# Holding the transposed loads of x behind the first chunk's copies, readying the gate column sooner, and loading the first two transposed chunks in one transfer

## The chip, the cores and the metric

The kernel runs on one core of one Trainium2 chip. The metric is the device time of one execution in microseconds (us).

## The reference, cut to what matters

```python
# A_x: (1, 2048, 640) bf16; the rows are worked on in 16 chunks of 128
def _A_ref(x, wqkv, wo):
    qkv = x @ wqkv                      # q, k, v, 32 heads of 20
    pq, pk = phi(q), phi(k)             # phi(t) = (t > 0 ? t + 1 : exp(t)) + 1e-6
    kv = einsum("bhsd,bhse->bhde", pk, v); z = sum of pk over s
    o = (pq @ kv) / (pq @ z + 1e-6)
    return o @ wo
def _B_ref(x, w1, w2, w3, w4): ...      # layernorm, gelu, shifted mixing, a second gelu block
g = sigmoid((x * gate_w).sum(-1))
return g * _A_ref(x) + (1 - g) * _B_ref(x)
```

The change touches only the first stage: k = x @ wk for each chunk of x, with the logit of the gate as one more column.

## The kernel before

In profiles and code, PE is TensorE (PEld its weight loads), DVE the vector engine, ACT the scalar engine; SP, and ACT as well, issue DMA transfers. A transfer lands when all its data have arrived. To evacuate a result is to take it out of PSUM, the memory that TensorE writes.

For k, TensorE needs each chunk of x transposed (xT). Chunks 0 and 1 are loaded plainly and transposed by TensorE itself (`turn`); DVE copies the results from PSUM into xT. Chunks 2 to 15 come transposed by DMA (`load_xT`). The weights wk come in five parts of 128 rows, by two issuing queues (SP and ACT).

```python
    load_x(0, 1)                                             # SP
    aq.dma_start(g5[:], gate_w.rearrange("(c p) -> c p", p=P))   # ACT
    load_wk(sp, 1)
    load_wk(aq, 0)
    load_x(1, 2, aq)
    load_wk(sp, 3)
    load_wk(aq, 2)
    load_wk(sp, 4)
    for c0, c1 in ((2, 3), (3, 4), (4, 6), (6, 8), (8, 12), (12, 16)):
        load_xT(c0, c1)                                      # SP, transposing
    sp.dma_start(wq_sb, wqkv_v[:, :, 0:D])
    load_x(2, 8)
    # ... cut: the other loads, all on SP
    # ... cut: constants
    def k_mm(pt, c, dcs, first=0, last=DC - 1):
        for dc in dcs:
            for hf in range(2):
                n = HD + hf                  # 320 and 321: the last column is the gate's logit
                nc.tensor.matmul(pt[:, hf, 0:n], lhsT=xT[:, dc, c * P:(c + 1) * P],
                                 rhs=wk_sb[:, dc, hf * HD:hf * HD + n], start=(dc == first), stop=(dc == last))
    # ... cut
    k0_order = (1, 0, 3, 4, 2)
    # ... cut: warmup(n, w) issues matmuls of constants, to bring TensorE to full pace
    turns = [(pair(), a, b) for a, b in ((0, 2), (2, DC))]

    def turn(c):
        for pt, a, b in turns:
            # ... cut: matmuls of x_sb[:, c, ...] against the identity
            if c == 0 and b == DC:
                nc.tensor.matmul(pt[:, 1, 0:DC], lhsT=g5z[:], rhs=ident[:, 0:DC], start=True, stop=True)
            nc.vector.tensor_copy(xT[:, a:b, c * P:(c + 1) * P], ...)
            if c == 0 and b == DC:
                nc.vector.tensor_copy(wk_sb[:, :, D], pt[:, 1, 0:DC])      # the gate column

    turn(0)
    warmup(1, TS)
    for n, dc in enumerate(k0_order):
        if n == 3:
            turn(1)
        elif 1 <= n < 3:
            warmup(1, 2 * P)
        k_mm(kp, 0, (dc,), first=k0_order[0], last=k0_order[-1])
    k_evac(kp, 0)
    for c in range(1, NCH):
        pt = pair()
        k_mm(pt, c, range(DC))
        k_evac(pt, c)
```

## Time and profile before

| | |
|---|---|
| time, median of 3 runs | 264.57 us (264.44 to 264.81) |
| span of the profiled execution | 262.6 us |
| TensorE busy | 98% of the span |
| first x transpose issued | 2.65 us |
| chunk 1's first k matmul | 6.99 us |
| chunk 2's first k matmul | 8.35 us |

The page of the kernel before: the first part gives the busy time of each engine with its share of the span, the fourth the share of the chain of work that ended last.

```profile
PE 257.9 (98%) x1719; PEld 160.0 (61%) x1738; DVE 142.7 (54%) x282; ACT 82.7 (31%) x123; POOL 20.2 (8%) x65
...
PE 98%; issue 0%; DVE 0%
```

TensorE is busy nearly everywhere, and the chain is TensorE's own order. So a change among the loads can only matter where TensorE waits for one of them. That is at the start. The next lines are the timeline of the kernel before: start, duration (both us; lines merge neighbours of one kind), engine, source line, operation, what it writes and reads, and in brackets the idle time before it with what ended it.

```profile
2.65 9.69 SPq L122 DMA_TRANSPOSE xT<-in_A_x_dram  x5
...
3.13 0.57 PEld L216 LDWEIGHTS <-x_sb 128*128 128x128 bf16 x5 [0.49 <-DMA x_sb<-in_A_x_dram]
...
3.69 0.89 DVE L219 CAST xT<-pp 128x256 bf16<-128x256 f32 x2 [1.28 <-PE pp L216]
...
4.22 0.93 PE L186 MATMUL pp<-wk_sb,xT 128*128 128x320 bf16 x2
4.49 0.17 DVE L222 CAST wk_sb<-pp 128x5 bf16<-128x5 f32 x1
...
5.15 0.68 PE L186 MATMUL pp<-wk_sb,xT 128*128 128x320 bf16 x2
...
5.77 0.44 PE L186 MATMUL pp<-wk_sb,xT 128*128 128x320 bf16 x2
6.08 0.28 PEld L214 LDWEIGHTS <-x_sb 128*128 128x128 bf16 x5 [0.20 <-DMA x_sb<-in_A_x_dram]
...
6.44 3.84 PE L186 MATMUL pp<-wk_sb,xT 128*128 128x320 bf16 x27
```

The six transposes are issued from 2.65 us on. The copy of the gate column (L222) ends at 4.66 us. TensorE transposes chunk 1 from 6.08 us, after a wait for its load, and from 6.44 us it runs k matmuls without a gap. Single records in the trace give the spacing: 320 columns take 0.27 us up to about 5.6 us and 0.136 us afterwards. I call these half and full pace. Chunk 1 then starts at 6.99 us and chunk 2 at 8.35 us. The pages have one trap: a matmul's record is about 300 ns long while matmuls start every 136 ns. So records overlap, and a short hole between them shows less idle time than it costs. Delays below are read from start to start.

### The profile page before, as it was taken

The numbers are of one execution on the slowest core, as the hardware profiler recorded it, in microseconds if no ns is written. First come the engines' busy times: TensorE is split into PE (matmuls) and PEld (weight loads), VectorE is DVE, ScalarE is ACT, GpSimd is POOL, SyncE is SP. The second block draws the span as 40 slices with busy tenths as digits, with TensorE's granted clock in tenths as the row PEclk, the third lists the DMA queues.
The fourth block names the chain that finished last, engine by engine and source line by source line (L and its number), as shares of the span: only waits on it lengthen the run. The fifth ranks groups of instructions, "written<-read, shape, count | busy, mean of one in ns | idle before, by whom it ended". The sixth has DMA issues, their size and how long they took to land.

```text
span 262.6 us, 4246 instructions
## 1 busy us (share of the span) xinstructions
PE 257.9 (98%) x1719; PEld 160.0 (61%) x1738; DVE 142.7 (54%) x282; ACT 82.7 (31%) x123; POOL 20.2 (8%) x65
## 2 busy tenths in 40 slices
PE   8999999999999999999999999999999999999995
PEld 4777555788755644555577555567565577555553
DVE  2788778899947998955403464413356223112132
ACT  1555554321166236522502222412131332142200
POOL 5000050012210040001000001000001000000000
DMA  7999987016682566600132000051100051100011
GB/s 204 197 171 379 364 248 304 0 27 125 125 99 58 111 121 167 235 0 2 25 75 77 25 0 2 0 100 52 50 0 2 1 100 52 50 0 2 0 50 50
DMA packets 45757, 23.98 MB, mean 91 GB/s; under 512 B 35114, under 2 KB 44970, under 8 KB 45738
## 3 DMA queue, kind: packets, MB, share of 16 engines
q1 hardware_dynamic: 45296, 23.22, 35.1%
q10 hardware_dynamic: 442, 0.49, 0.5%
q8 instruction: 13, 0.21, 0.4%
q14 instruction: 6, 0.05, 0.1%
HBM read 12.21 MB, written 2.62 MB: 56 GB/s over the span
## 4 chain that ended last, share of the span: by engine, by line
PE 98%; issue 0%; DVE 0%
PE pp L500 22%; PE pp L467 21%; PE pp L186 9%; PE pp L315 8%; PE pp L451 8%; PE pp L420 8%; PE pp L349 8%; PE pp L243 8%; PE pp L199 1%; PE pp L387 1%; PE pp L475 1%; PE pp L509 1%; PE pp L368 1%; PE pp L258 0%; PE pp L216 0%
## 5 line engine op out<-in xcount | busy, mean ns | idle before, releaser
L467 PE MATMUL pp<-lnxT,w_sb 128*128 128x512 bf16 x249 | 59.8, 379 | 0.6
L500 PE MATMUL pp<-w_sb,h 128*128 128x384 bf16 (+3 forms) x414 | 57.6, 299 | 0.2 <-issue 0.2
L469 ACT ACTIVATE h<-pp 128x1024 bf16<-128x1024 f32 (+1 forms) x28 | 26.9, 961 | 82.2 <-PE pp L467 82.2
L500 PEld LDWEIGHTS <-h 128*128 128x128 bf16 x416 | 38.3, 98 | 19.3 <-issue 1.1
L467 PEld LDWEIGHTS <-w_sb 128*128 128x128 bf16 x260 | 25.4, 98 | 26.8
L514 DVE SCALAR_TENSOR_TENSOR oc<-pp,omg,x 128x640 bf16<-128x640 f32 (+2 forms) x20 | 14.4, 748 | 45.1 <-ACT h2x L478 21.3
L454 DVE SCALAR_TENSOR_TENSOR x<-pp,gate,x 128x640 f32<-128x640 f32 x16 | 13.9, 868 | 29.4 <-PE pp L451 29.4
L178 ACT ACTIVATE e<-pp 128x640 bf16<-128x640 f32 (+1 forms) x26 | 21.5, 826 | 9.6 <-PE pp L243 9.6
L451 PE MATMUL pp<-m_sb,pqT 128*128 128x320 bf16 x160 | 24.3, 299 | 0.0
L420 PE MATMUL pp<-w_sb,hsT 128*128 128x320 bf16 x160 | 23.9, 299 | 0.0
L423 DVE TENSOR_TENSOR x<-pp,x_sb 128x640 f32<-128x640 f32 x16 | 13.1, 820 | 19.7 <-PE pp L420 19.7
L186 PE MATMUL pp<-wk_sb,xT 128*128 128x320 bf16 (+1 forms) x160 | 23.1, 303 | 0.0
L315 PE MATMUL pp<-x_sb,pk 128*128 128x320 bf16 (+1 forms) x160 | 22.0, 300 | 0.0
L243 PE MATMUL pp<-xT,hsT 128*128 128x512 bf16 x98 | 21.6, 379 | 0.1
L315 PEld LDWEIGHTS <-pk 128*128 128x128 bf16 x160 | 18.8, 117 | 3.2
L420 PEld LDWEIGHTS <-hsT 128*128 128x128 bf16 x160 | 15.7, 98 | 8.2
L451 PEld LDWEIGHTS <-pqT 128*128 128x128 bf16 x160 | 15.7, 98 | 7.7
L186 PEld LDWEIGHTS <-xT 128*128 128x128 bf16 x160 | 15.7, 99 | 6.5 <-DVE xT L219 0.2
L349 PE MATMUL pp<-lnxT,w_sb 128*128 128x512 bf16 x76 | 17.9, 379 | 0.2
L243 PEld LDWEIGHTS <-hsT 128*128 128x128 bf16 x100 | 11.8, 118 | 9.7
L285 POOL TENSOR_SCALAR rstd<-mv 128x4 f32<-128x4 f32 (+1 forms) x11 | 3.4, 312 | 153.6 <-DVE mv L291 153.6
L180 DVE SCALAR_TENSOR_TENSOR pk<-pp,e 128x640 bf16<-128x640 f32 x16 | 13.2, 825 | 1.7
(76 smaller groups left out, 189.9 us busy)
## 6 DMA issues: line engine op xcount, KB each, us to landing
out_dram<-oc SPq DMA_DIRECT2D x14, 160.0 KB, 1.8
w_sb<-in_B_w_dram SPq DMA_DIRECT2D x1, 2160.0 KB, 8.4
w_sb<-in_B_w_dram SPq DMA_DIRECT2D x1, 2080.0 KB, 9.9
x_sb<-in_A_x_dram SPq DMA_DIRECT2D x1, 1280.0 KB
x_sb<-in_A_x_dram SPq DMA_DIRECT2D x1, 960.0 KB, 7.4
wo_sb<-in_A_wo_dram SPq DMA_DIRECT2D x6, 160.0 KB, 7.8
hsT<-in_A_wqkv_dram SPq DMA_DIRECT2D x1, 800.0 KB, 5.1
m_sb<-in_A_wqkv_dram SPq DMA_DIRECT2D x1, 800.0 KB, 12.0
```

The source lines that it names most:

```text
L178: nc.scalar.activation(ev, src, ACT.Exp)
L186: nc.tensor.matmul(pt[:, hf, 0:n], lhsT=xT[:, dc, c * P:(c + 1) * P], rhs=wk_sb[:, dc, hf * HD:hf * HD + n], start=(dc == first), stop=(dc ...
L243: nc.tensor.matmul(pt[:, t % 2, :], lhsT=wq_sb[:, dc, :].rearrange("p (m j) -> p j m", j=DC)[:, j], rhs=xT[:, dc, t * TS:(t + 1) * TS], st ...
L315: nc.tensor.matmul(pt[:, hf, 0:HD + hf], lhsT=w, rhs=x_sb[:, c, hf * HD:(hf + 1) * HD + hf], start=(c == 0), stop=(c == NCH - 1))
L349: nc.tensor.matmul(pt[:, i, :], lhsT=w, rhs=lnxT[t][:, dc, :], start=(dc == 0), stop=(dc == DC - 1))
L420: nc.tensor.matmul(pt[:, hf, 0:HD], lhsT=hsT[:, fc, 2 + c * P:2 + (c + 1) * P], rhs=w2_sb[:, fc, hf * HD:(hf + 1) * HD], start=(fc == 0), ...
L451: nc.tensor.matmul(pt[:, hf, 0:HD], lhsT=pqT[:, j, c * P:(c + 1) * P], rhs=m_sb[:, j, hf * HD:(hf + 1) * HD], start=(j == 0), stop=(j == D ...
L454: nc.vector.scalar_tensor_tensor(x1, pt[:, :, 0:HD], gate[:, c:c + 1], x1, op0=ALU.mult, op1=ALU.add)
L467: nc.tensor.matmul(pt[:, k, :], lhsT=w3_sb[:, dc, fc * P:(fc + 1) * P], rhs=lnT[:, dc, :], start=(dc == 0), stop=(dc == DC - 1))
L469: nc.scalar.activation(h2[:, 2 * i * TS:(2 * i + n) * TS], pt[:].rearrange("p h e -> p (h e)")[:, 0:n * TS], ACT.Gelu_apprx_tanh)
L500: nc.tensor.matmul(dst, lhsT=st[t]["h2"][:, fc * TS + cc * P:fc * TS + (cc + 1) * P], rhs=w4_sb[:, fc, a:b], start=start and fc == 0, stop ...
L514: nc.vector.scalar_tensor_tensor(oc[:, a:b], src, omg[:, c:c + 1], st[t]["x1"][cc][:, a:b], op0=ALU.mult, op1=ALU.add)
```

## The change

The intent: keep the transposes and all later loads off the DMA engines until chunk 0's first copies are done, so that the plain loads at the start are not disturbed; get the gate column ready sooner; and bring chunks 2 and 3 in one transfer (chunks 8 to 11, one transfer before, become two pairs). The hold is a one-column memset inside chunk 2's place in xT. The transpose that overwrites it must wait for DVE, and everything behind it on the SP queue waits too.

```diff
-    for c0, c1 in ((2, 3), (3, 4), (4, 6), (6, 8), (8, 12), (12, 16)):
-        load_xT(c0, c1)
-    sp.dma_start(wq_sb, wqkv_v[:, :, 0:D])
-    ... (the later loads)
+
+    def late_loads():
+        for c0, c1 in ((2, 4), (4, 6), (6, 8), (8, 10), (10, 12), (12, 16)):
+            load_xT(c0, c1)
+        sp.dma_start(wq_sb, wqkv_v[:, :, 0:D])
+        ... (the later loads, in the same order)
@@ in turn(c)
-            if c == 0 and b == DC:
+            if c == 0 and a == 0:
                 nc.tensor.matmul(pt[:, 1, 0:DC], lhsT=g5z[:], rhs=ident[:, 0:DC], start=True, stop=True)
             nc.vector.tensor_copy(xT[:, a:b, c * P:(c + 1) * P], ...)
-            if c == 0 and b == DC:
+            if c == 0 and a == 0:
                 nc.vector.tensor_copy(wk_sb[:, :, D], pt[:, 1, 0:DC])
+                nc.vector.memset(xT[:, 0:1, 2 * P:2 * P + 1], 0.0)
 
     turn(0)
+    late_loads()
+    ... (POOL's copies of w1, which need a late load, moved here unchanged)
     warmup(1, TS)
```

More of the change, by code (lines that the diff above doesn't have):

```diff
@@ L134 @@
     load_wk(sp, 4)
-    for c0, c1 in ((2, 3), (3, 4), (4, 6), (6, 8), (8, 12), (12, 16)):
-        load_xT(c0, c1)
-    sp.dma_start(wq_sb, wqkv_v[:, :, 0:D])
-    load_x(2, 8)
-    load_x(8, 16)
-    sp.dma_start(wv_sb[:], wqkv_v[:, :, 2 * D:3 * D])
-    sp.dma_start(w1_sb[:], B_w1.rearrange("(c p) f -> p c f", p=P))
-    for g in range(NG):
-        sp.dma_start(wo_sb[:, g, :], A_wo[row0[g]:row0[g] + P, :])
-    for g in range(4):
-        sp.dma_start(w2_sb[:, g, :], B_w2[CG * g:CG * g + P, :])
-        sp.dma_start(w2_sb[32 * g:32 * (g + 1), 4, :], B_w2[CG * g + P:CG * (g + 1), :])
-    sp.dma_start(w3_sb[:], B_w3.rearrange("(c p) f -> p c f", p=P))
+    def late_loads():
+        for c0, c1 in ((2, 4), (4, 6), (6, 8), (8, 10), (10, 12), (12, 16)):
+            load_xT(c0, c1)
+        sp.dma_start(wq_sb, wqkv_v[:, :, 0:D])
+        load_x(2, 8)
+        load_x(8, 16)
+        sp.dma_start(wv_sb[:], wqkv_v[:, :, 2 * D:3 * D])
+        sp.dma_start(w1_sb[:], B_w1.rearrange("(c p) f -> p c f", p=P))
+        for g in range(NG):
+            sp.dma_start(wo_sb[:, g, :], A_wo[row0[g]:row0[g] + P, :])
+        for g in range(4):
+            sp.dma_start(w2_sb[:, g, :], B_w2[CG * g:CG * g + P, :])
+            sp.dma_start(w2_sb[32 * g:32 * (g + 1), 4, :], B_w2[CG * g + P:CG * (g + 1), :])
+        sp.dma_start(w3_sb[:], B_w3.rearrange("(c p) f -> p c f", p=P))
     nc.gpsimd.memset(mhalf[:], -0.5)
@@ L167 @@
         nc.gpsimd.memset(kvT[:, b:b + 2], 0.0)
-    for dc in range(DC):
-        for g in range(4):
-            nc.gpsimd.tensor_copy(w1x[:, dc, 32 * g:32 * (g + 1)], w1_sb[:, dc, CG * g + P:CG * (g + 1)])
     def phi(dst, src, n):
@@ L220, in turn @@
                                   ptb[:, 0:(b - a) * P].rearrange("p (c s) -> p c s", c=b - a))
-            if c == 0 and b == DC:
+            if c == 0 and a == 0:
                 nc.vector.tensor_copy(wk_sb[:, :, D], pt[:, 1, 0:DC])
+                nc.vector.memset(xT[:, 0:1, 2 * P:2 * P + 1], 0.0)
     turn(0)
+    late_loads()
+    for dc in range(DC):
+        for g in range(4):
+            nc.gpsimd.tensor_copy(w1x[:, dc, 32 * g:32 * (g + 1)], w1_sb[:, dc, CG * g + P:CG * (g + 1)])
     warmup(1, TS)
```

## The prediction

> **What bounds it now.** TensorE. The page's first part has PE busy 257.9 of 262.6 us, and the chain that ended last is 98% PE. Later stages are dense, so the change can act only on the first ten microseconds and on when the transposed chunks arrive.
>
> The timeline of the first 9 us shows:
> - x chunk 0 lands at 3.1 us; its identity matmuls run 3.2 to 3.8 us, then two DVE casts (423 and 547 ns) and a 169 ns copy of the gate column into wk_sb (4.49 to 4.66 us).
> - The first chunk's second matmul needs that column and starts only at 4.72 us, 0.5 us after the first. Matmuls run at half pace until about 5.6 us (320 columns every 0.27 us, later every 0.136).
> - Chunk 1's transposes start at 6.08 us, when x chunk 1 lands. From 6.99 us PE is unbroken at 1.36 us a chunk: chunk 2 at 8.35 us, chunk 4 at 11.1.
>
> The x transposes are issued at 2.65, 4.0, 5.3, 6.8, 8.5 and 12.4 us. Chunk 2 lands near 6.45 us (3.8 after issue), chunk 3 at 7.8, chunks 4-5 at 9.7 (4.4 after issue), 6-7 at 12.0: 1.3 to 1.9 us of slack. In the trace's packets the transposes start to move at 5.3 us and share the engines with the last 100 or so of 896 row packets of the plain loads.
>
> **What the change does.**
> 1. The gate-column matmul and copy move to the first half of chunk 0: ready near 4.4 us instead of 4.66, PE gains 0.25 us. The second cast ends 0.45 us later (near 5.0), needed near 5.5: free.
> 2. A one-column DVE memset (0.1 us) in chunk 2's place makes the first transpose wait: issued near 4.6 us instead of 2.65, with all that is behind it on the SP queue.
> 3. Without transposes in the way x chunk 1 and the last two wk parts (6.03, 6.40, 6.58 us) land about 0.3 us sooner. PE would reach chunk 2 at 8.1 us: the gain of 0.25 us is kept.
> 4. Chunks 2-3 come in one transfer. Chunks 4-5 took 4.4 us behind a backlog; single lnxT chunks later, without traffic, take 2.6. My estimate for the pair is 3.6 to 4.4 us, landing 8.2 to 9.0. Chunk 2's slack is spent: PE waits 0.1 to 0.9 us, most likely 0.5.
> 5. Later pairs, issued every 1.55 us, land near 10.4, 12.5, 14.5 and 16.5 us, needed near 11.2, 14, 16.7, 19.4: no second wait. The queue gets to wq near 17 us as now (16.7; wq lands at 21.8, needed at 27.4).
>
> **Sum.** -0.25 us from the gate column, +0.5 us from the wait at chunk 2: about +0.2 us. A wait under 1 us should not bring back the half pace: the Trainium skill ("TensorE: Matmul & The Clock Gate", Part 1) has the clock drop after an idle window of about 3.4 us. The trace before has no such idle stretch to test it on.
>
> **Predicted 264.7 us, 8 in 10 within 263.9 to 265.5.** Chances: faster by over 2% 0.01, within 2% 0.98, slower by over 2% 0.01.
>
> **What would show it.** First transpose issued near 4.6 us; second matmul of chunk 0 near 4.5; x chunk 1 landing near 5.7; PE idle some 0.5 us before chunk 2, released by the x transpose; no other gap; later stages shifted as one block.
>
> **What would make it wrong.** If the pair lands in 3.4 us there is no wait and the time is about 264.3. If it takes over 5 us, the wait exceeds 1 us and half pace might come back, costing a microsecond or more. TensorE reaching full pace sooner or later because its start changed: half a microsecond either way.

## The result, and the profile after

The changed kernel took 264.53 us (median of 6 runs, 264.46 to 264.74), the kernel before 264.38 us (6 runs, 264.24 to 264.81). The ratio is 1.0006, with a 95% interval of 0.9993 to 1.0018: the same. Ratios here are the mean time of one kernel's runs over that of the other's of the same rounds, so they are not quite the ratio of the medians quoted.

The page after, the same parts:

```profile
PE 259.1 (99%) x1738; PEld 159.9 (61%) x1738; DVE 142.7 (54%) x283; ACT 82.7 (31%) x123; POOL 20.2 (8%) x65
...
PE 97%; DMA 2%; DVE 0%; issue 0%
PE pp L504 22%; PE pp L471 21%; PE pp L319 8%; PE pp L455 8%; PE pp L424 8%; PE pp L353 8%; PE pp L247 8%; PE pp L185 7%; DMA xT<-in_A_x_dram 2%; PE pp L391 1%; PE pp L479 1%; PE pp L198 1%; PE pp L513 1%; PE pp L372 1%; PE pp L262 0%; DVE xT L218 0%
```

The chain that ended last now holds 2% of DMA: followed back, TensorE's order at one point runs into the landing of an x transpose. The 1.2 us more of TensorE busy time is no extra work. The trace before has 1,719 matmuls recorded and this one 1,738, with 1,738 weight loads in both, so some records were missing before.

The timeline after, the lines that answer to those of before:

```profile
3.11 0.28 PEld L215 LDWEIGHTS <-x_sb 128*128 128x128 bf16 x2 [0.47 <-DMA x_sb<-in_A_x_dram]
...
4.04 0.17 DVE L221 CAST wk_sb<-pp 128x5 bf16<-128x5 f32 x1
...
4.16 0.06 DVE L222 MEMSET xT<- 128x1 bf16 x1
...
4.26 6.49 SPq L122 DMA_TRANSPOSE xT<-in_A_x_dram  x4
4.44 0.69 PE L185 MATMUL pp<-wk_sb,xT 128*128 128x320 bf16 x2
...
5.14 0.53 PE L185 MATMUL pp<-wk_sb,xT 128*128 128x320 bf16 x2
...
5.63 0.43 PE L185 MATMUL pp<-wk_sb,xT 128*128 128x320 bf16 x2
5.86 0.31 PEld L213 LDWEIGHTS <-x_sb 128*128 128x128 bf16 x5
...
6.18 2.17 PE L185 MATMUL pp<-wk_sb,xT 128*128 128x320 bf16 x14
...
8.54 2.02 PEld L185 LDWEIGHTS <-xT 128*128 128x128 bf16 x16 [0.53 <-DMA xT<-in_A_x_dram]
8.55 2.22 PE L185 MATMUL pp<-wk_sb,xT 128*128 128x320 bf16 x15 [0.19 <-DMA xT<-in_A_x_dram]
```

The first transpose is issued at 4.26 us, right behind the memset at 4.16. The gate column is ready at 4.21 us. Chunk 1 (inside the line that starts at 6.18 us) starts at 6.83 us, 0.16 us earlier than before. Then TensorE stops. The lines at 8.54 and 8.55 us are chunk 2, and its weight load waited 0.53 us for an x transpose. Start to start that matmul came 494 ns after the one before it instead of 137, a loss of 0.36 us. So chunk 2 starts 0.20 us later than before (8.55 against 8.35 us), and from there on every stage is moved by the same amount: the last k matmul starts at 27.50 us against 27.29, and the span is 262.82 us against 262.61.

### The profile page after: what moved, and what is told of

It reads as the page before. It is cut to its first block, busy times and chain, and to the rows that moved or that the text cites. A ratio compares the mean times of both kernels' runs of the same rounds, so it can differ in the third digit from the quotient of the medians.

```text
span 262.8 us, 4268 instructions
## 1 busy us (share of the span) xinstructions
PE 259.1 (99%) x1738; PEld 159.9 (61%) x1738; DVE 142.7 (54%) x283; ACT 82.7 (31%) x123; POOL 20.2 (8%) x65
## 4 chain that ended last, share of the span: by engine, by line
PE 97%; DMA 2%; DVE 0%; issue 0%
PE pp L504 22%; PE pp L471 21%; PE pp L319 8%; PE pp L455 8%; PE pp L424 8%; PE pp L353 8%; PE pp L247 8%; PE pp L185 7%; DMA xT<-in_A_x_dram 2%; PE pp L391 1%; PE pp L479 1%; PE pp L198 1%; PE pp L513 1%; PE pp L372 1%; PE pp L262 0%; DVE xT L218 0%
## 5 line engine op out<-in xcount | busy, mean ns | idle before, releaser
L471 PE MATMUL pp<-lnxT,w_sb 128*128 128x512 bf16 x260 | 60.4, 379 | 0.0
L353 PE MATMUL pp<-lnxT,w_sb 128*128 128x512 bf16 x80 | 18.1, 379 | 0.0
```

Of the source, the lines that this page charges most:

```text
L353: nc.tensor.matmul(pt[:, i, :], lhsT=w, rhs=lnxT[t][:, dc, :], start=(dc == 0), stop=(dc == DC - 1))
L471: nc.tensor.matmul(pt[:, k, :], lhsT=w3_sb[:, dc, fc * P:(fc + 1) * P], rhs=lnT[:, dc, :], start=(dc == 0), stop=(dc == DC - 1))
```

## The experiments

The theory after the result: the first part of the change wins a little before chunk 1, and the hold makes chunk 2's data late, which takes it back. Rivals: (1) the 0.16 us at chunk 1 did not come from the gate column at all, but from the loads, the clock or chance; (2) the wait at chunk 2 comes from the pair's longer transfer and not from the hold.

This table has what the single records of each kernel's one trace show, in us. "Full pace" is the start of the first k matmul that is followed by another within 0.15 us; the clock records, where a trace has them, put the change itself 0.1 to 0.7 us earlier. "Last wk" is the landing of the last wk part. "Transpose" is the issue of the first x transpose. The last two columns are the median time, and that of the kernel before in the same rounds.

| kernel | full pace | last wk | chunk 1 | transpose | chunk 2 | last k matmul | time | before |
|---|---|---|---|---|---|---|---|---|
| before | 5.77 | 6.58 | 6.99 | 2.65 | 8.35 | 27.29 | 264.38 | |
| changed | 5.63 | 6.52 | 6.83 | 4.26 | 8.55 | 27.50 | 264.53 | 264.38 |
| changed, again (e11) | 4.79 | 6.91 | 7.22 | 4.26 | 8.66 | 27.61 | 264.64 | 264.43 |
| gate column alone (e1) | 5.24 | 6.71 | 7.05 | 2.66 | 8.42 | 27.35 | 264.39 | 264.43 |
| hold, chunks split as before (e2) | 5.02 | 6.43 | 6.74 | 4.26 | 8.10 | 27.50 | 264.68 | 264.43 |
| pair and gate column, no hold (e3) | 5.66 | 6.46 | 6.86 | 2.65 | 8.22 | 27.16 | 264.55 | 264.43 |
| hold to x chunk 0 (e6) | 4.18 | 6.41 | 6.79 | 3.24 | 8.15 | 27.09 | 264.49 | 264.43 |
| hold to x chunk 1 (e12) | 6.50 | 6.29 | 7.05 | 5.84 | 9.89 | 28.84 | 266.28 | 264.43 |
| hold to chunk 1's copies (e4) | 4.43 | 6.31 | 6.74 | 6.43 | 10.91 | 31.52 | 268.26 | 264.47 |
| hold to chunk 1's evacuation (e5) | 4.86 | 6.53 | 6.84 | 10.51 | 15.06 | 35.61 | 272.87 | 264.47 |

### e1: the gate column alone

```diff
 (on the kernel before)
-            if c == 0 and b == DC:      (twice)
+            if c == 0 and a == 0:
```

> The kernel before with only the gate-column matmul and copy moved to the first half of chunk 0; transposes early and split as before. Theory A (the gate column made chunk 1 start 0.16 us earlier in the changed kernel, and the wait for the pair of chunks took it back): gate copy done near 4.2 us, chunk 1's matmuls start near 6.8 us and chunk 2 near 8.2 us with no wait, 0.15 to 0.25 us faster than before. Rival B (the 0.16 us came from TensorE reaching full pace earlier in that one execution, or from undisturbed loads, not from the gate column): chunk 1 starts near 7.0 us, chunk 2 near 8.35, time equal to before within 0.1 us.

Measured: 264.39 us (264.04 to 264.88) against 264.43 (263.95 to 265.63), ratio 0.9996 (0.9979 to 1.0014). The gate column was ready at 4.21 us, as in the changed kernel, but chunk 1 started at 7.05 us. The timeline of e1 shows what TensorE was waiting for instead:

```profile
4.63 0.66 PE L186 MATMUL pp<-wk_sb,xT 128*128 128x320 bf16 x2 [0.20 <-DMA wk_sb<-in_A_wqkv_dram]
...
6.51 5.75 PE L186 MATMUL pp<-wk_sb,xT 128*128 128x320 bf16 x41 [0.18 <-DMA wk_sb<-in_A_wqkv_dram]
```

It waited for a wk part at 4.63 us and for another at 6.51 us. Making the column ready earlier gained nothing, since the weights were not there. In this one trace the first wk part was also later than before (landed 4.59 us, against 4.17), so e1 alone does not show what the column is worth; the trace of e3 does, below. Rival 1 stands.

### e2: the hold, with the chunks split as before

```diff
 (on the changed kernel)
-        for c0, c1 in ((2, 4), (4, 6), (6, 8), (8, 10), (10, 12), (12, 16)):
+        for c0, c1 in ((2, 3), (3, 4), (4, 6), (6, 8), (8, 12), (12, 16)):
```

> The changed kernel with the transfer sizes of before (chunks 2 and 3 each alone), hold kept. If the wait at chunk 2 comes from the pair's longer transfer: chunk 2 lands about 3.8 us after an issue near 4.3, at 8.1, the wait falls from about 0.5 us to under 0.1, and the time is 0.2 to 0.35 us under the changed kernel's. If it comes from the hold alone: chunk 2 still lands near 8.5 us and the time stays with the changed kernel's. A wait may move to chunk 3 (needed 1.36 us after chunk 2, issued 1.3 us after it).

Measured: 264.68 us (264.55 to 265.06), ratio 1.0009 (0.9993 to 1.0026). Both expectations were too simple. Chunk 2 had no wait (8.10 us), nor had chunk 3. But TensorE then waited for x transposes twice further on, as the waits of e2 show (who waited for what: us in total, times, longest):

```profile
PEld L185 <- DMA xT<-in_A_x_dram: 0.8, 2, 0.4
```

The matmul records put these waits at chunk 4 (347 ns from start to start instead of 137) and at chunk 8. The last k matmul came at 27.50 us, to 0.01 us the same as in the changed kernel. That match is partly chance: chunk 1 was 0.09 us earlier here, and the two waits cost 0.44 us, not 0.36. The transfers follow one another from one queue, so delaying the first delayed the others: chunks 4 and 5 landed at 10.99 us instead of 9.72 before, chunks 8 to 11, one transfer again in e2, at 16.68 instead of 16.44 (needed at 16.52 before, so next to no slack there). How chunks are grouped chooses which of them pays. Rival 2 falls as the source of the loss: the pair decides that chunk 2 is the one to wait, the hold that one must (e3, next, has the pair without the hold and no wait).

### e3: the pair and the early gate column, without the hold

```diff
 (on the changed kernel)
-                nc.vector.memset(xT[:, 0:1, 2 * P:2 * P + 1], 0.0)
 (and late_loads() called where the loads stood before the change)
```

> The changed kernel without the hold (memset removed, later loads issued at 2.65 us as before), pair and early gate column kept. Theory A: the pair lands near 7.0 us, PE does not wait at chunk 2, chunk 2 starts near 8.2 us, 0.15 to 0.25 us faster than before and about 0.35 us faster than the changed kernel. If the hold is what made the plain loads and hence chunk 1 early, then chunk 1 starts near 7.0 us and the time equals before.

Measured: 264.55 us (264.20 to 265.00), ratio 1.0003 (0.9985 to 1.0021). In the trace TensorE waits nowhere for a transpose; chunk 2 starts at 8.22 us and the last k matmul at 27.16 us, 0.34 us ahead of the changed kernel, as expected. The times don't resolve it: the runs of this kernel spread over 0.8 us. Chunk 1 started at 6.86 us without any hold, so the hold was not what made it early.

This trace is also the clean test of the gate column. The first wk part was there in time (3.95 us), and chunk 0's second matmul started at 4.49 us instead of 4.72: the 0.23 us that the prediction had counted on. But chunk 0 then had to wait for wk part 4, which landed at 6.28 us, and chunk 1 started 0.12 us earlier than before, by just as much as that part was earlier (6.28 against 6.40).

### e6: a shorter hold

```diff
 (on the changed kernel)
-                nc.vector.memset(xT[:, 0:1, 2 * P:2 * P + 1], 0.0)
 
+    nc.vector.tensor_copy(xT[:, 0:1, 2 * P:2 * P + 1], x_sb[:, 0:1, 0:1])
+    late_loads()
     turn(0)
-    late_loads()
```

> The changed kernel with a shorter hold: the first transpose waits for a one-element DVE copy that waits for x chunk 0 (landing at 3.1 us), so it is issued near 3.4 us, not 4.26. If landing follows issue at about 4.2 us, the pair lands near 7.6 us, before PE needs it near 8.2: no wait, and about 0.35 us faster than the changed kernel, 0.15 to 0.25 faster than before. If landing is set by when the plain loads' packets have drained (transposes moved at 5.3 us in the kernel before although issued at 2.65), the pair lands near 7.6 to 8.2 us all the same, with little or no wait.

Measured: 264.49 us (264.12 to 265.46), ratio 1.0007 (0.9986 to 1.0028). The transpose was issued at 3.24 us and there was no wait at chunk 2 (8.15 us); the last k matmul started at 27.09 us. That is what was expected of the trace. The expected gain in time did not show, again within a spread larger than it. Why the times of e3 and e6 do not follow their traces is not settled; each kernel has one trace, and the starts of its other executions are not seen.

### e12, e4, e5: longer holds

Each moves only the point at which DVE releases the transposes. e12 waits for x chunk 1's landing, e4 for chunk 1's copies, e5 for chunk 1's evacuation.

```diff
 (on the changed kernel; its memset and its call of late_loads() removed)
 e12, before warmup(1, TS):
+    nc.vector.tensor_copy(xT[:, 0:1, 2 * P:2 * P + 1], x_sb[:, 1:2, 0:1])
+    late_loads()
 e4, after turn(1):
+            nc.vector.memset(xT[:, 0:1, 2 * P:2 * P + 1], 0.0)
+            late_loads()
 e5, after k_evac(pt, c):
+        if c == 1:
+            nc.vector.memset(xT[:, 0:1, 2 * P:2 * P + 1], 0.0)
+            late_loads()
```

> The changed kernel with a hold between the two long ones and its own: the first transpose waits for a one-element copy that waits for x chunk 1's landing (5.4 to 5.8 us), so it is issued near 5.7 us. With 4.3 to 4.5 us from issue to landing, chunk 2 is reached by its data near 10.1 us, TensorE idle for about 1.7 us. If half pace comes back only after more idle than that (it did after 2.65 us idle), the time is about 1.6 us over before, 266.0; with half pace, about 267.5.

> The changed kernel with a longer hold: the one-column memset comes after chunk 1's copies instead of after chunk 0's first copy, so the first transpose is issued near 6.9 us instead of 4.26. If the wait at chunk 2 is the hold's and landing follows issue at about 4.2 us, the pair lands near 11.1 us, TensorE waits about 2.8 us before chunk 2 (about 0.4 in the changed kernel), and the time is about 267.0 us, 2.4 us over the changed kernel's. If the queue of plain loads set the landing, the pair would land earlier, near 9.5 to 10 us, and the time rise by only about 1 us. If half pace comes back already with such a wait, matmuls after it are 0.27 us apart and another microsecond or more is added.

> The changed kernel with a hold until chunk 1's evacuation (memset near 10.4 us, first transpose issued near 10.5). The pair lands near 14.7 us and TensorE waits about 6.5 us before chunk 2. If the clock keeps its pace the time is about 270.7 us; if half pace comes back after an idle stretch of about 3.4 us, as the Trainium skill (TensorE: Matmul & The Clock Gate, Part 1) has it, chunk 2 runs at 0.27 us a matmul and up to 1.7 us more are lost: about 272.4 us.

Measured: e12 266.28 us (ratio 1.0080, 1.0065 to 1.0094), e4 268.26 (1.0136, 1.0116 to 1.0155), e5 272.87 (1.0321, 1.0305 to 1.0337). Chunk 2 was expected near 10.1, 11.1 and 14.7 us in this order, and started at 9.89, 10.91 and 15.06. The issue of the transposes and the k matmuls after the wait, from the timelines of e12, e4 and e5:

```profile
5.84 6.36 SPq L122 DMA_TRANSPOSE xT<-in_A_x_dram  x4
...
9.89 2.35 PE L185 MATMUL pp<-wk_sb,xT 128*128 128x320 bf16 x16 [1.31 <-DMA xT<-in_A_x_dram]
```

```profile
6.43 6.27 SPq L122 DMA_TRANSPOSE xT<-in_A_x_dram  x4
...
10.91 1.34 PE L185 MATMUL pp<-wk_sb,xT 128*128 128x320 bf16 x5 [2.65 <-DMA xT<-in_A_x_dram]
```

```profile
10.51 6.31 SPq L122 DMA_TRANSPOSE xT<-in_A_x_dram  x4
...
15.06 1.50 PE L185 MATMUL pp<-wk_sb,xT 128*128 128x320 bf16 x5 [6.70 <-DMA xT<-in_A_x_dram]
```

In all kernels whose transposes came too late, TensorE reached chunk 2 between 4.05 and 4.55 us after the issue: 4.29 and 4.40 in the two traces of the changed kernel, 4.05 in e12, 4.48 in e4, 4.55 in e5. From the changed kernel to e5 the issue moved by 6.25 us and chunk 2 by 6.51. So the wait follows the hold nearly one for one.

The second reading is the pace. From chunk 2's start to the last k matmul it is 18.94 us in the kernel before (27.29 less 8.35, before rounding), 18.95 in e12, but 20.61 in e4 and 20.55 in e5. In e4 the matmuls after the wait were 267 ns apart until 14.5 us. The windows of e4 show it in the clock (columns: window and its length, busy time and count of each engine, granted TensorE clock, DMA share, GB/s):

```profile
10.00:12.00 2.00, 1.09 (x5) 0.68 (x6) 0.35 (x1) 0.00 (x0) 0.00 (x0) 0.78 1.17 205
12.00:14.00 2.00, 2.00 (x9) 1.14 (x8) 0.00 (x0) 0.38 (x2) 0.00 (x0) 0.50 1.22 224
14.00:16.00 2.00, 2.00 (x15) 1.34 (x14) 1.15 (x2) 0.88 (x3) 0.00 (x0) 0.87 1.03 191
```

The clock record has it at half from 11.1 to 14.5 us. So 2.65 us of idle time brought half pace back in e4's trace, and it cost 1.7 us (20.61 less 18.94). In e12, 1.31 us of idle time did not. The Trainium skill ("TensorE: Matmul & The Clock Gate", Part 1) says the clock drops after an idle window of about 3.4 us; in this trace it dropped at the end of a stretch of 3.41 us (7.69 to 11.11 us) of which only 2.65 us were idle. In every trace with more than one recorded change of the clock, the changes lie whole multiples of 3.413 us apart (4.28, 11.11 and 14.52 us in e4). Counted on from e12's change at 6.19 us, such a step falls at 9.60 us and cuts its idle time in two. So it may matter where an idle time falls among these steps, and not only how long it is; that is inferred from the traces and was not tested. Of the four runs of e4, two show a mean granted clock of 0.994 (268.55 and 268.68 us) and two of 1.0 (267.62 and 267.96). So with this idle time the drop seems to come in some executions and not in others. The two without it (spans of 265.9 and 266.2 us) are still 3.3 and 3.6 us longer than the 262.6 of the kernel before, more than the wait of e4's trace explains; they have no trace, and this stays open. The added time of e4's trace is accounted for: chunk 2 started 2.56 us later than before and the slow matmuls cost 1.67, which makes 4.23; the span grew by 4.24 us (266.85 less 262.61).

### e9 and e13: without the last wk part

These two are one kernel, run twice. The result is wrong: the last plain load is left out and part 0 of wk is used for part 2.

```diff
 (on the kernel before)
-    load_wk(aq, 2)
-                                 rhs=wk_sb[:, dc, hf * HD:hf * HD + n], ...
+                                 rhs=wk_sb[:, dc if dc != 2 else 0, hf * HD:hf * HD + n], ...
```

> Wrong result on purpose: the kernel before with the last plain load (wk part 2, 160 KB of 1,120) left out and part 0 used in its place. If chunk 1's start is bound by the landing of the last wk parts (it came 0.31 to 0.41 us after wk part 2 landed in all six traces so far), then the remaining last part lands near 6.0 to 6.1 us, chunk 1 starts near 6.6 us instead of 6.99, and the time falls by about 0.3 us. If the gate column or the clock binds it, chunk 1 still starts near 6.9 us or later and the time does not move.

> Wrong result on purpose, the same kernel without the last wk part again: in its first trace TensorE came to full pace only near 7 us (by 5.8 in all others), which hid what the missing part does. If full pace comes by 5.8 us this time and the last wk parts bind the start, chunk 1's matmuls start near 6.6 us (6.83 to 7.05 with all parts) and the last k matmul near 26.9 us. If they start near 6.8 or later, the wk parts do not bind.

Measured in e9: 264.36 us (ratio 0.9999, 0.9983 to 1.0014). Its profiled execution was no use for the question: full pace came only at 7.05 us, and chunk 1 started at 7.59. Measured in e13: 264.01 us (0.9991, 0.9979 to 1.0003). Full pace came at 5.05 us, the last remaining part landed at 6.04 us, and chunk 1 started at 6.62 us, the last k matmul at 26.93. Both are within 0.03 us of what was expected if the last wk parts bind, and 6.62 us is the earliest of all kernels that work on chunk 0 alone first; but the margin is smaller than the expectation says, which leaves out e2, e4 and e6 (6.74 to 6.79 us with all parts). This is one trace; the time's interval just includes no change.

```profile
6.08 6.16 PE L185 MATMUL pp<-wk_sb,xT 128*128 128x320 bf16 x44
```

The line starts at 6.08 us, right after the landing of the last part; its first four matmuls finish chunk 0.

### e11: the changed kernel again

> The changed kernel again, unchanged, for the spread. If the wait at chunk 2 is a fixed cost of the hold, TensorE again waits 0.2 to 0.6 us before chunk 2, whichever time full pace comes, and the median is 0 to 0.3 us over before. If the wait was that one execution's accident, chunk 2 starts without one.

Measured: 264.64 us (264.42 to 266.06), ratio 1.0017 (1.0000 to 1.0034). In this trace the last wk part landed at 6.91 us, chunk 1 started at 7.22 us, and the wait at chunk 2 had shrunk: its first matmul came 212 ns after the one before, 0.08 us more than usual. This falls short of the 0.2 us expected. The waits of e11:

```profile
PE pp L185 <- DMA wk_sb<-in_A_wqkv_dram: 0.7, 2, 0.4
...
PEld L185 <- DMA xT<-in_A_x_dram: 0.2, 1, 0.2
```

So the wait is not a fixed cost. What the hold fixes is the time at which chunk 2 can start, 8.55 us in one trace and 8.66 in the other. When the plain loads are late, TensorE arrives late and waits little; when they are early, it waits for the difference.

### e8 and e10: a try for a better version

If the wk parts bind the start, TensorE could use the time by working on chunks 0 and 1 together, part by part, instead of on warm-up matmuls.

```diff
 (on the kernel before, with the gate column in the first half)
+    load_x(1, 2, aq)            (ahead of the wk parts)
...
-    for n, dc in enumerate(k0_order):
-        ... (turn(1), warm-up matmuls, k_mm of chunk 0)
+    k0_order = (1, 3, 0, 4, 2)
+    k_mm(kp, 0, (1,), first, last)
+    turn(1)
+    k_mm(kp, 0, (3,), first, last)
+    k_mm(k1, 1, (1, 3), first, last)
+    for dc in (0, 4, 2):
+        k_mm(kp, 0, (dc,), first, last)
+        k_mm(k1, 1, (dc,), first, last)
 (e10 as well)
-    for c0, c1 in ((2, 3), (3, 4), (4, 6), (6, 8), (8, 12), (12, 16)):
+    for c0, c1 in ((2, 3), (3, 4), (4, 6), (6, 8), (8, 10), (10, 12), (12, 16)):
```

> A try for a better version: the kernel before with early transposes, the gate column in the first half, x chunk 1 loaded ahead of the wk parts, and the matmuls of chunks 0 and 1 interleaved by wk part in place of the warm-up matmuls. If wk landings (to about 6.5 us) bind the start, both chunks are done about 0.6 us after the last part lands plus what is left at half pace, near 7.6 to 8.0 us instead of 8.35: 0.35 to 0.7 us faster than before if the transposed chunks are in time (chunk 2 lands near 6.5, chunk 4 near 9.7, needed near 10.4). If TensorE then gets to full pace later because the warm-up matmuls are gone, the gain is lost. If x chunk 1 first delays wk parts 1 and 0 by 0.5 us or more, the gain is under 0.2 us.

> The interleaved kernel with one edit: chunks 8 to 11 come as two pairs instead of one transfer of four. In the interleaved kernel's trace chunk 2 started 0.44 us earlier than before (7.91 against 8.35 us), but TensorE waited about 0.33 us at chunk 8 for the four-chunk transfer (landed 16.36). With pairs, chunks 8 and 9 should land near 14 us and the wait vanish: the last k matmul starts near 26.85 us (27.19 interleaved, 27.29 before), the time 0.3 to 0.5 us under before. If each transfer's landing is set by the queue behind it, the wait moves to chunk 10 or 12 and nothing is gained.

Measured: e8 264.22 us (263.95 to 264.66), ratio 0.9992 (0.9980 to 1.0005). In its trace chunk 2 started at 7.91 us, 0.44 us ahead of before, but TensorE then waited for the four-chunk transfer at chunk 8, and the last k matmul came at 27.19 us, only 0.10 us ahead. e10, meant to remove that wait, took 265.43 us (264.23 to 267.28), ratio 1.0046 (1.0010 to 1.0082): three runs at 264.2 to 264.5 and three at 266.4 to 267.3. Its profiled execution was one of the shorter ones (264.47 us). In it the last wk part landed at 7.20 us, TensorE waited 0.9 us for wk parts, and the last k matmul came at 27.35. What the three long runs lost is not in any trace and stays open. No version here beats the kernel before beyond doubt.

## Why the prediction was right, and where it was not

The time was right: 264.7 us was predicted and 264.53 measured, with "within 2%" held likely. That alone says little: the predicted range, 263.9 to 265.5 us, also holds the 264.38 of the kernel before. Point by point:

- **The hold makes chunk 2 late: right.** The pair was put at 8.2 to 9.0 us. TensorE could go on at 8.55 us, and at 8.66 in the second trace. The most likely wait, 0.5 us, was 0.36 us start to start in the first trace (0.53 on the weight loads) and 0.08 in the second. The long holds confirm the cause: chunk 2 moved with the issue nearly one for one. One reading behind it was wrong: chunk 2's landing before, put near 6.45 us. That trace gives no landing for the first transpose, and I had used the next one's 3.8 us. In e9 and e13, whose transposes are those of before (with one plain load fewer ahead of them), it landed at 6.76 and 6.72 us, so the slack was at most about 1.6 us, not 1.9. It was probably less: with that load gone the packets of the transposes start to move at 4.99 and 4.86 us, against 5.31 before.
- **No second wait, one block shifted, wq in time: right.** After chunk 2 no transpose was waited for. The wq load was issued at 16.31 us and landed at 21.68.
- **The gate column gains 0.25 us: this step failed.** The column was ready at 4.21 us, as predicted or better, but the wk part for the first matmul landed at 4.40 us. The second matmul started at 4.66 us instead of the predicted 4.5; before it was 4.72. e1, which has only this part, gained nothing. In e3, where it did land in time, the second matmul gained 0.23 us, and none of it was left at chunk 1. What binds instead is one of the last two wk parts, of which chunk 0 uses part 4 first and then part 2: part 4 in the traces of before, e1, e3, e4 and e6, part 2 in those of the changed kernel (both), e2 and e5. In each, the matmul that needs it starts 0.04 us after it lands. (In the kernel before, x chunk 1 was nearly as late: TensorE was transposing it until 6.37 us, part 4 landed at 6.40.) Counted from the landing of part 2, the last, chunk 1 came 0.31 to 0.43 us later in the traces of before, of the changed kernel (both), and of e1 to e6; only in e12, where full pace came as late as 6.50 us, was it 0.76 us. e13, without part 2, has part 4 landing at 6.04, its matmul at 6.08 and chunk 1 at 6.62 us. The mistake was to take what one early matmul waited for (the gate column, at 4.72 us) as the limit of the whole start, although weights that chunk 0 also needs landed up to 1.9 us later.
- **The plain loads land 0.3 us sooner: mis-sized.** The last wk part landed at 6.58, 6.71 and 6.46 us in the traces whose transposes were issued at 2.65 (before, e1, e3), and at 6.52, 6.91, 6.43, 6.31, 6.53 and 6.29 in those with the hold of 4.26 us or longer (changed, e11, e2, e4, e5, e12). The means are 6.58 and 6.50 us. The difference of 0.08 us is far below the spread of 0.6 us. The packets show how little the transposes were in the way: although issued at 2.65 us, they start to move only at 5.31 us in the kernel before, when 90 of the 896 row packets of the plain loads are left. In the changed kernel they start at 5.67 us with 16 left, so a hold of 1.6 us at the issue moved them by 0.36 us.
- **The net of +0.2 us:** chunk 2 started 0.20 us later than before in the first trace and 0.31 in the second (8.66 less 8.35). The kernel without the hold (e3) got there at 8.22. The sum was right with terms that were not, which is in part luck: the gain before chunk 1 was not the gate column's and was absent in the second trace, and the wait then shrank with it, since chunk 2's start is set by the hold.
- **The wait does not bring half pace back: right** for the changed kernel, and the reason given was close. Idle times of 1.31 us (e12) did not bring it back, 2.65 us (e4) did, in its trace.

What stays open: whether the changed kernel is slower at all in time. Both traces and the second ratio (1.0017) lean that way, the first ratio (1.0006) includes no change, and 0.2 us is 0.08% of the time.

## What to carry to other kernels

A transfer that has slack can be held back for free only up to that slack. Here it was at most 1.6 us for chunk 2, 1.35 for chunks 4 and 5 (landed 9.72, needed 11.07 us before) and about 0.1 for the one transfer of chunks 8 to 11 (16.44 and 16.52), the hold took 1.6, and splitting the transfers only moved the wait from one chunk to another. Before speeding up the operation that a matmul was seen to wait for, look for the input that lands last before the stage runs dense. A single trace cannot separate 0.2 us from the scatter of load landings and of the clock at the start; a second trace of the same kernel, or one experiment that exaggerates the effect, can.

## What the Trainium skill lacked or had wrong

- "TensorE: Matmul & The Clock Gate", Part 1: the clock is said to drop after an idle window of about 3.4 us. In e4's trace it dropped at the end of a stretch of 3.41 us of which 2.65 us were idle (2.95 us from matmul start to matmul start), so the stretch need not be idle from end to end; half pace was then recorded for 3.4 us. The 1.31 us of e12 did not bring it. Two of e4's four runs show the lower mean clock.
- The same page, Part 1, has the change to full pace vary by 0.5 us either way with the phase of a free-running window. Here, with warm-up matmuls from 0.83 us on in every kernel, the clock records put it between 4.06 us (e6) and 6.74 us (e9). The warm-up is not unbroken, as the page's example is: in e9 no matmul started between 3.84 and 4.80 us.
- The same page, Part 1, warns that recorded clock events are not to be trusted fully. Here the recorded changes agree with the spacing of the matmuls around them, in the eleven traces that have any. What misleads is a missing record: the traces of the kernel before, e3 and e8 hold none, and the windows then print a clock of 1.00, as for the kernel before from 4 to 6 us, where its matmuls start 0.27 us apart until about 5.6 us.
- "DMA: Bandwidth & Descriptors" gives a bandwidth for transposing transfers; I found no latency there. Here 256 rows of 640 bf16 from HBM took 4.05 to 4.55 us from issue until TensorE could go on, early in the kernel, and a four-chunk transfer kept the issuing queue busy for 3.8 and 4.3 us against 1.5 to 1.6 for a pair (before).
